# Scores of two heads as 64-row products, with the mask added on TensorE

## The chip, the cores and the metric

The kernel runs on one core of a Trainium2 chip. The metric is the device time of one launch in microseconds (us). The kernel before takes 739.22 us, the median of three runs (739.21 to 739.76).

## The reference

Local attention with a memory, and a gated MLP behind it. q, k and v are 4 batches x 8 heads x 576 tokens x 64 features, in float32.

```python
scores = q @ k.T / 8                      # causal, later keys at -1e9
local  = softmax(scores) @ v
q_p    = where(q > 0, q, exp(q) - 1) + 1
mem    = (q_p @ M_prev) / (q_p . z_prev + 1e-6)
x      = sigmoid(beta) * mem + (1 - sigmoid(beta)) * local     # 2304 x 512
out    = ((x @ w_a) * (x @ w_b)) @ w_out                       # d_ff = 1536
```

## The kernel before

Every float32 product is made of three products of split numbers: x = hi + lo, and x * y = hi * hi + hi * lo + lo * hi.

**Attention** works on a pair of heads, A and B, at a time; there are 16 pairs. The queries of a head lie in four tiles of 128 tokens (0 to 3), and the last 64 tokens of both heads share one tile (4). The work on a pair is cut into named steps, and the string `ORDER` (L21) is the order of all steps within one iteration, written by hand as `step:lag`: in iteration i a step works on pair i - lag. So an iteration holds steps of up to four pairs, and each engine runs its part of them strictly in that order. An iteration is what repeats; the first ones lack the late steps, and the last ones the early steps.

The steps that the change and the prediction touch:

- `TK`, `TQ`, `Tq` (L395) turn k and q on TensorE into feature layout; `th` (L409, ScalarE) copies the hi part out of PSUM and `tl` (L416, VectorE) the lo part. The result is `f`, with head A on partitions 0 to 63 and head B on 64 to 127: `f[0]` holds q's hi and k's lo, `f[1]` q's lo and k's hi.
- `D_` (L422) copies `f` by four DMAs into `two`, where the two parts of one head stand over each other on 128 partitions. Pair 0 has no `two`.
- `S_A`, `S_B` (tiles 0 and 1 of a head, in one PSUM bank), `S_2A`, `S_2B`, `S_3A`, `S_3B` (tiles 2 and 3) and `S_4` (L449) are the scores. A tile of a head takes one 64-row product of `f` (L459) and one 128-row product of `two` (L462), which holds the other two terms. Pair 0 takes three 64-row products. Tile 4 takes six products (L470).
- `m` (L483, VectorE) adds the mask, a bf16 tile as wide as the scores, and takes the row minimum in the same pass; the pass leaves the minimum in an accumulator, and a second short instruction reads it. Of tiles 0 and 1 the masked scores go to SBUF (tile `P`), of the others back to PSUM.
- `e` (L495, ScalarE) takes the exponential, from SBUF or PSUM, and sums it.
- `r_` and `n` (VectorE, GpSimd) scale the rows; `G` (L531, TensorE) turns the probabilities; `h`, `l` (L565, L590) split them to hi and lo; `V` (L602) multiplies them with v; `x` (L623) takes the result out.

Beside these, iterations hold steps of the memory's part of x: those of a token tile (`ma`, `mb`, `mu`, `mc`, `md`, `me`; 6 tiles, the work of VectorE) in iterations 2 to 7 and a little behind, those of a pair's features (`pa` to `py`; 8 of them, with products on TensorE) behind these.

PSUM has eight banks: six are the tiles `pt` of one pool (`ps_t`, L271), which the steps T, S, G, pa and pe take in turn, each waiting until a bank's last reader is done; two make one wide tile `pw` for S_4 and V.

**The MLP** (L736 on) follows. Its weights come as two words of a float64 and are put together by VectorE, ScalarE and GpSimd while the first columns run on TensorE; from then on TensorE works alone. The change does not touch it, but for the order of its first steps in the last iterations.

Of the kernel before, what the change touches and what calls it, by code (L numbers as in the profile page):

```python
# [22 lines left out]
S_2A:1 hi0:3 clamp2:3 S_2B:1 pf:3 cx:3 lo0:3 r_:2 V1A:3 sm:0 V2A:3 thK:0 high3:3 shift2:3 thQ:0  # L23
tlK:0 pa:2 e3A:1 ma:0 mag4:3 xA:3 Tq:0 pd:2 tlQ:0 clamp4:3 m2A:1 thq:0 mb:0 pb:2 high2:3 m2B:1
clamp1:2 S_3B:1 mag3:2 e2A:1 shift1:2 H0:3 shift4:3 S_A:1 e2B:1 m3B:1 n2:2 clamp0:2 V1B:3 low2:3
high1:2 e3B:1 mA:1 shift0:2 pc:2 V2B:3 n4:2 G2B:2 tlq:0 mx:3 S_B:1 hi2:3 G2A:2 xB:3 mu:0 md:2
n1:2 D_:0 low3:3 h2B:2 Lt:-1 high4:3 clamp3:2 h2A:2 low4:3 eA:1 n3:2 low1:2 high0:2 hi1:2
shift3:2 G5:2 n0:2 G1:2 S_4:1 lo2:3 h5:2 v_h:2 Lp:1 mB:1 h1:2 low0:2 l2B:2 G4:2 h4:2 l2A:2 Lv:1
hh:3 Lk:-2 G0:2 G3A:2 h0:2 lo1:2 v_l:2 hl:3 w_0:2 LM:0 st_:3 l0:2 h3A:2 me:2 px:3 G3B:2 h3B:2
m4:1 l5:2 py:3  # L30
# [1135 lines left out]
```

## Time and profile before

| what | before |
|---|---|
| median of three runs | 739.22 us |
| the profiled execution, first to last instruction | 736.9 us |
| what lies around that span, against the median | 2.3 us |
| TensorE busy | 706.5 us (96%), 3861 products |
| VectorE busy | 487.5 us (66%) |
| ScalarE busy | 326.9 us (44%) |
| GpSimd busy | 256.1 us (35%) |
| mean granted clock of TensorE | 0.984 |

A busy TensorE is not one at its peak: a product is shown from its start until its result has landed, and the next starts long before that. What a product takes from the engine is the distance from its start to the next one's start. Attention ends at about 230 us and its last steps at about 252 us of the span, the weights are done at about 369 us, and the rest is the MLP alone.

### The profile page before, as it was taken

The numbers are of one execution on the slowest core, as the hardware profiler recorded it, in microseconds if no ns is written. First come the engines' busy times: TensorE is split into PE (matmuls) and PEld (weight loads), VectorE is DVE, ScalarE is ACT, GpSimd is POOL, SyncE is SP. The second block draws the span as 40 slices with busy tenths as digits, with TensorE's granted clock in tenths as the row PEclk, the third lists the DMA queues.
The fourth block names the chain that finished last, engine by engine and source line by source line (L and its number), as shares of the span: only waits on it lengthen the run. The fifth ranks groups of instructions, "written<-read, shape, count | busy, mean of one in ns | idle before, by whom it ended". The sixth has DMA issues, their size and how long they took to land.

```text
span 736.9 us, 11356 instructions
## 1 busy us (share of the span) xinstructions
PE 706.5 (96%) x3861; PEld 627.2 (85%) x3861; DVE 487.5 (66%) x1128; ACT 326.9 (44%) x821; POOL 256.1 (35%) x359
## 2 busy tenths in 40 slices
PE   7999999999998897978899999999999999999998
PEld 6777778778877886878799999999999999999997
DVE  6889999877888999999966754445444454441111
ACT  5787877877777544444332222222222222221111
POOL 1687887778678533333361020000100010000000
PEclk9799999999999998999999999999999999999999
DMA  7999989989985354344214231112111121001001
GB/s 164 213 206 196 236 192 214 229 173 203 226 216 172 103 173 144 123 150 147 79 58 97 44 98 23 31 25 71 41 30 32 54 56 32 1 3 41 1 0 44
DMA packets 129465, 79.98 MB, mean 109 GB/s; under 512 B 98816, under 2 KB 117248, under 8 KB 129408
## 3 DMA queue, kind: packets, MB, share of 16 engines
q1 hardware_dynamic: 129408, 79.26, 44.4%
q8 instruction: 31, 0.51, 0.3%
q14 instruction: 26, 0.21, 0.1%
HBM read 49.35 MB, written 14.16 MB: 86 GB/s over the span
## 4 chain that ended last, share of the span: by engine, by line
PE 76%; DVE 16%; ACT 3%; issue 2%; DMA 1%; SPq 1%; POOL 1%; DVEq 0%
PE pp L840 30%; PE o L877 15%; PE pt L89 8%; PE pw L618 6%; PE pt L462 6%; PE pt L459 6%; DVE wt L778 4%; DVE wt L785 3%; DVE wt L771 3%; PE pw L470 1%; DVE wt L764 1%; PE m L1013 1%; ACT hh L859 1%; DVE hl L93 1%; POOL P L518 1%
## 5 line engine op out<-in xcount | busy, mean ns | idle before, releaser
L840 PE MATMUL pp<-xh,wh 128*128 128x384 f32 x568 | 194.1, 342 | 16.1 <-ACT x L852 15.3
L840 PE MATMUL pp<-xh,wl 128*128 128x384 f32 x568 | 192.7, 339 | 0.0
L840 PE MATMUL pp<-xl,wh 128*128 128x384 f32 x568 | 192.3, 338 | 0.0
L840 PEld LDWEIGHTS pp<-xh,wh 128*128 128x128 f32 x568 | 108.0, 190 | 23.5 <-ACT x L852 20.1
L855 DVE TENSOR_TENSOR x<-pp,x 128x384 f32<-128x384 f32 x71 | 39.3, 553 | 122.7 <-ACT x L852 122.5
L840 PEld LDWEIGHTS pp<-xl,wh 128*128 128x128 f32 x568 | 108.1, 190 | 2.6
L840 PEld LDWEIGHTS pp<-xh,wl 128*128 128x128 f32 x568 | 108.0, 190 | 0.0
L852 ACT ACTIVATE x<-pp 128x384 f32<-128x384 f32 x71 | 34.4, 484 | 124.6 <-PE pp L840 124.6
L518 POOL TENSOR_SCALAR P<-P,sum 128x384 f32<-128x384 f32 (+2 forms) x144 | 81.7, 590 | 22.2 <-DVE sum L510 21.7
L1005 POOL TENSOR_TENSOR xx<-xx 128x384 f32<-128x384 f32 x16 | 16.7, 1042 | 200.9 <-DMA xx<-xs 158.1
L877 PE MATMUL o<-wh,hl 128*128 128x512 f32 x216 | 85.5, 396 | 0.0
L877 PE MATMUL o<-wl,hh 128*128 128x512 f32 x216 | 85.0, 393 | 0.0
L877 PE MATMUL o<-wh,hh 128*128 128x512 f32 x216 | 84.9, 393 | 0.0
L93 POOL TENSOR_TENSOR wl<-wt,wh 128x512 fp32r<-128x512 f32 x32 | 45.5, 1421 | 77.4 <-DVE hl L93 39.3
L93 DVE TENSOR_TENSOR hl<-x,hh 128x384 fp32r<-128x384 f32 x71 | 40.5, 571 | 42.0 <-ACT hh L859 42.0
L859 ACT ACTIVATE hh<-x 128x384 fp32r<-128x384 f32 x72 | 37.8, 525 | 63.0 <-DVE x L855 63.0
L93 DVE TENSOR_TENSOR PT<-pt,PT 128x512 fp32r<-128x512 f32 (+2 forms) x112 | 60.7, 588 | 2.1 <-ACT PT L573 1.1
L573 ACT ACTIVATE PT<-pt 128x512 fp32r<-128x512 f32 (+2 forms) x112 | 52.6, 513 | 17.0 <-PE pt L89 17.0
L618 PEld LDWEIGHTS pw<-PT,vh 128*128 128x128 f32 x416 | 57.1, 189 | 2.0 <-POOL PT L93 1.2
L89 PE MATMUL pt<-ident,P 128*128 128x128 f32 (+1 forms) x400 | 55.5, 282 | 3.1 <-POOL P L518 3.0
L618 PE MATMUL pw<-PT,vh 128*128 128x320 f32 (+4 forms) x416 | 56.3, 285 | 1.8 <-POOL xh L251 1.0
L462 PE MATMUL pt<-two 128*128 128x128 f32 (+2 forms) x120 | 50.9, 424 | 2.3 <-DMA two<-f 2.3
(128 smaller groups left out, 1191.1 us busy)
## 6 DMA issues: line engine op xcount, KB each, us to landing
two<-f SPq DMA_DIRECT2D x60, 256.0 KB, 4.4
xs<-xo SPq DMA_DIRECT2D x16, 576.0 KB, 4.8
xx<-xs SPq DMA_DIRECT2D x48, 192.0 KB, 3.4
...
```

The lines of the kernel that those rows point to most:

```text
L89: nc.tensor.transpose(out, x, ident[0:x.shape[0], 0:x.shape[0]])
L93: eng.tensor_tensor(out=lo, in0=x, in1=hi, op=ALU.subtract)
L459: nc.tensor.matmul(o, lhsT=f[0][r, qc], rhs=f[1][r, kc], start=True, stop=False)
L462: nc.tensor.matmul(o, lhsT=t[:, qc], rhs=t[:, kc], start=False, stop=(t is lows[-1]))
L518: nc.gpsimd.tensor_scalar(out=pr[:, h, :], in0=pr[:, h, :], scalar1=r[:, c:c + 1], scalar2=1.0, op0=ALU.mult, op1=ALU.mult,)
L573: nc.scalar.activation(out=dst, in_=src, func=AF.Copy)
L618: nc.tensor.matmul(pv[:, a:hi], lhsT=w, rhs=x, start=(n == 0), stop=(n == len(ops) - 1))
L840: nc.tensor.matmul(pp, lhsT=w[:, w0:w0 + P], rhs=x[:, kk, :], start=(c == 0), stop=(c == 3 * KK - 1),)
L852: nc.scalar.activation(out=x, in_=ps[1], func=AF.Copy)
L855: nc.vector.tensor_tensor(out=h[0], in0=ps[0], in1=h[0], op=ALU.mult)
L859: nc.scalar.activation(out=h[1], in_=h[0], func=AF.Copy)
L877: nc.tensor.matmul(po[t, m], lhsT=hx[:, m * P:(m + 1) * P], rhs=w[:, w0:w0 + DM], start=(f == 0 and n == 0), stop=(f == NFT - 1 and n == 2),)
```

## The change

- A tile's scores are three 64-row products in place of one 64-row and one 128-row product, and `D_`, `two` and their DMAs are gone.
- The steps of A and B become one: `S_`, `S_2` and `S_3` make both heads' tiles, and the products alternate between A, on rows 0 to 63, and B, on rows 64 to 127. Each head's tile has its own bank, so a step takes two.
- The mask is added by a product: `ident_b` (a bf16 identity) times `mask` (128 x 128), into the last 128 columns of each tile of 0 to 3, and `mask_t` (64 columns) of tile 4.
- `m` is a plain row minimum of VectorE, read from PSUM; nothing is written back, and there is no second instruction. `e` reads all scores from PSUM.
- The order string is made anew.

```diff
 ORDER = """
-l1:3 e4:2 eB:2 l4:3 mc:1 mag2:3 pe:3 H1:3 mag1:2 l3A:3 TK:0 l3B:3 S_3A:1 mag0:2 m3A:1 TQ:0
...
+mc:1 l1:3 e4:2 l4:3 eB:2 H1:3 S_3:1 pe:3 mag1:2 l3A:3 TK:0 l3B:3 m3A:1 mag2:3 m3B:1 TQ:0 hi0:3
...
-        @steps("")
-        def D_(s, b, j, part):
-            if s is st[0]:
-                return
-            two = s["two"] = p2_e.tile([P, 2, 2 * FULL], F32R, tag="two", name="two")
-            for n in range(2):
-                for h in range(2):
-                    nc.sync.dma_start(
-                        out=two[64 * n:64 * n + 64, h, :].bitcast(F32),
-                        in_=s["f"][n][64 * h:64 * h + 64, 0:2 * FULL].bitcast(F32),
-                    )
...
-        @steps(*PARTS)
+        def add_product(o, w, x, first=False):
+            nc.tensor.matmul(o, lhsT=w, rhs=x, start=first, stop=True, skip_group_check=True)
+
+        @steps("", "2", "3")
         def S_(s, b, j, part):
...
+            f, tiles = s["f"], []
+            for h in "AB":
+                s["S", part + h] = psum()
+                tiles.append(list(scores(s, part + h)))
+                for i, *_, o in tiles[-1]:
+                    add_product(o[:, i * P:], ident_b, mask, i != 1)
+            for two in zip(*tiles):
+                for w, x in ((f[0], f[1]), (f[0], f[0]), (f[1], f[1])):
+                    for i, h, _, o in two:
+                        r = slice(64 * h, 64 * h + 64)
+                        add_product(
+                            o, w[r, i * P:(i + 1) * P], x[r, FULL:FULL + P * (i + 1)]
                         )
...
+        @steps(str(NF))
+        def S_(s, b, j, part):
+            s["S", part] = wide(S, HALF)
+            (*_, o), = scores(s, part)
+            f, qd = s["f"], s["qd"]
+            add_product(o[:, FULL:S], ident_b, mask_t, True)
...
         def m(s, b, j, part):
...
-            for i, h, c, src in scores(s, part):
-                nc.vector.tensor_tensor_reduce(
-                    out=masked(s, i, h, src), in0=src,
-                    in1=mask_t if i == NF else mask[:, FULL - (i + 1) * P:],
-                    scale=1.0, scalar=FAR, op0=ALU.add, op1=ALU.min, accum_out=s["nm"][:, c:c + 1],
-                )
...
+            for _, _, c, src in scores(s, part):
+                nc.vector.tensor_reduce(out=s["nm"][:, c:c + 1], in_=src, axis=AX.X, op=ALU.min)
...
                 nc.scalar.activation(
-                    out=s["P", i][:, h, :], in_=masked(s, i, h, src), func=AF.Exp, scale=-1.0,
+                    out=s["P", i][:, h, :], in_=src, func=AF.Exp, scale=-1.0,
                     bias=s["nm"][:, c:c + 1], accum_out=s["sum"][:, c:c + 1],
                 )
```

What the change does to the order, at three places. TensorE before, in an iteration of the middle, from the turning of the next pair's k (`kr`) on: S_3A, then the turning of q (`qr`), S_2A and S_2B, then V (`pw<-PT,vh`).

```order
L89 MATMUL pt<-ident,kr 128x128 x4
L459 MATMUL pt<-f_2634,f_2633 128x512
L462 MATMUL pt<-two 128x512
L89 MATMUL pt<-ident,qr 128x128 x4
L459 MATMUL pt<-f_2634,f_2633 128x384
L462 MATMUL pt<-two 128x384
L459 MATMUL pt<-f_2634,f_2633 128x384
L462 MATMUL pt<-two 128x384
L618 MATMUL pw<-PT_2718,vh 128x256
```

TensorE now, the same place: S_3 of both heads with its two mask products, a step of the memory (L239), k and q, and V; S_2 stands behind V.

```order
L436 LDWEIGHTS ident_b
L436 MATMUL pt<-mask,ident_b 128x128
L436 LDWEIGHTS ident_b
L436 MATMUL pt<-mask,ident_b 128x128
L436 MATMUL pt<-f_2545,f_2544 128x512 x2
L436 MATMUL pt<-f_2544 128x512 x2
L436 MATMUL pt<-f_2545 128x512 x2
L239 MATMUL pt<-nh,md_203 128x384
L239 MATMUL pt<-nl,md_203 128x384
L239 MATMUL pt<-nh,md_203 128x384
L88 MATMUL pt<-ident,kr 128x128 x4
L88 MATMUL pt<-ident,qr 128x128 x4
```

The 64-row products of a step now stand together, six at a time, where a 64-row and a 128-row product took turns; S_3A and S_3B, which stood half an iteration apart, are one step at its start.

ScalarE before, from the hi copies of the next pair's k and q (`f<-pt`) to the exponentials of tiles 0 and 1 of head A.

```order
L413 ACTIVATE f_2634<-pt 128x512
L413 ACTIVATE f_2633<-pt 128x512
L499 ACTIVATE P_2603,sum<-pt,nm 128x512
L627 ACTIVATE xo<-pw 128x576
L413 ACTIVATE f_2634<-pt 128x64
L413 ACTIVATE qdiag_102<-pt 64x64 x2
L223 ACTIVATE nh<-pt 128x384
L499 ACTIVATE P_2651,sum<-pt,nm 128x384 x2
L499 ACTIVATE P_2603,sum<-pt,nm 128x512
L627 ACTIVATE xo<-pw 128x576
L573 ACTIVATE PT_2718<-pt 128x3x128 x2
L499 ACTIVATE P_2678,sum<-P_2678,nm 128x128
```

ScalarE now, the same stretch.

```order
L412 ACTIVATE f_2769<-pt 128x512
L412 ACTIVATE f_2768<-pt 128x512
L484 ACTIVATE P_2788,sum<-pt,nm 128x512
L612 ACTIVATE xo<-pw 128x576
L484 ACTIVATE P_2788,sum<-pt,nm 128x512
L222 ACTIVATE nh<-pt 128x384
L412 ACTIVATE f_2769<-pt 128x64
L412 ACTIVATE qdiag_102<-pt 64x64 x2
L484 ACTIVATE P_2828,sum<-pt,nm 128x384 x2
L612 ACTIVATE xo<-pw 128x576
L558 ACTIVATE PT_2866<-pt 128x3x128 x2
L484 ACTIVATE P_2880,sum<-pt,nm 128x128
```

The second exponential of tile 3 (512 columns) moved ahead, and those of tiles 0 and 1 read `pt`, a PSUM bank, where they read `P` in SBUF. Next, SyncE's queue of an iteration before.

```order
L631 DMA xs<-xo 256x1x576
L428 DMA two<-f_2421 64x1024 x2
L428 DMA two<-f_2422 64x1024 x2
L211 DMA xx<-xs 64x2x384 x2
L330 DMA vr<-in_v_dram 128x4x64 x2
```

And SyncE's queue of an iteration now.

```order
L616 DMA xs<-xo 256x1x576
L329 DMA kr<-in_k_dram 128x4x64 x2
L329 DMA qr<-in_q_dram 128x4x64 x2
L210 DMA xx<-xs 64x2x384 x2
L329 DMA vr<-in_v_dram 128x4x64 x2
```

The four copies into `two` are gone, and the loads of k and q stand directly behind the store of `xo`.

## Rows read from the trace of the kernel before

**Rows 1.** Busy time by stretch, first line says what the columns are.
```profile
core 0: us, PE busy (x) PEld busy (x) DVE busy (x) ACT busy (x) POOL busy (x), PEclk, DMA share, GB/s
44.25:113.06 68.81, 68.27 (x417) 54.52 (x416) 65.15 (x182) 57.40 (x171) 57.28 (x88) 1.00 0.97 208
...
113.06:230.00 116.94, 116.17 (x721) 93.66 (x720) 95.11 (x275) 91.65 (x272) 88.84 (x146) 1.00 0.87 193
...
252.00:369.00 117.00, 101.32 (x499) 91.85 (x499) 108.53 (x157) 50.41 (x94) 43.18 (x32) 0.96 0.43 138
```
**Rows 2.** Timeline of TensorE, scores in one iteration: start us, us, engine, line, what.
```profile
173.67 0.60 PE L89 MATMUL pt<-ident,kr 128*128 128x128 f32 x4
174.20 0.49 PE L459 MATMUL pt<-f,f 64*128 64x512 f32 x1
...
174.96 0.60 PE L89 MATMUL pt<-ident,qr 128*128 128x128 f32 x4
175.49 0.44 PE L459 MATMUL pt<-f,f 64*128 64x384 f32 x1
...
176.89 0.28 PE L618 MATMUL pw<-PT,vh 128*128 128x256 f32 x1
...
183.35 0.32 PE L459 MATMUL pt<-f,f 64*128 64x128 f32 x1
...
184.40 0.27 PE L89 MATMUL pt<-ident,P 128*128 128x128 f32 x1
```
**Rows 3.** Timeline of TensorE, the scores of pair 0 (64-row products alone).
```profile
10.11 0.49 PE L459 MATMUL pt<-f,f 64*128 64x512 f32 x1
...
11.00 0.66 PE L89 MATMUL pt<-ident,qr 128*128 128x128 f32 x4
11.59 0.45 PE L459 MATMUL pt<-f,f 64*128 64x384 f32 x2
...
12.21 0.21 PE L400 MATMUL pt<-ident,kt 64*128 64x64 f32 x1
...
12.66 0.47 PE L459 MATMUL pt<-f,f 64*128 64x512 f32 x1
...
14.22 1.08 PE L470 MATMUL pw<-f,qdiag 128*128 128x288 f32 x6
```
**Rows 4.** Groups of ScalarE from 113 to 230 us: xcount, busy us, mean ns.
```profile
L627 ACT ACTIVATE xo<-pw 128x576 f32<-128x576 f32 x16 | 10.4, 651 | 16.7 <-PE pw L618 16.7
L499 ACT ACTIVATE P<-pt,nm 128x384 f32<-128x384 f32 x16 | 9.1, 580 | 0.0
L499 ACT ACTIVATE P<-P,nm 128x256 f32<-128x256 f32 x17 | 8.6, 508 | 0.0
L573 ACT ACTIVATE PT<-pt 128x384 fp32r<-128x384 f32 x16 | 7.8, 489 | 6.5 <-PE pt L89 6.5
L499 ACT ACTIVATE P<-P,nm 128x128 f32<-128x128 f32 x16 | 6.5, 404 | 0.0
```
**Rows 5.** Timeline of ScalarE, two copies of 512 columns behind each other.
```profile
173.08 1.07 ACT L573 ACTIVATE PT<-pt 128x512 fp32r<-128x512 f32 x2
```
**Rows 6.** Groups of VectorE, a masked row minimum and a row sum, both of 384 columns.
```profile
L487 DVE CUSTOM_DVE_ANT_0 pt<-pt,mask 128x384 f32<-128x384 f32 x32 | 17.3, 567 | 0.0
...
L986 DVE TENSOR_REDUCE n<-q 128x12 f32<-128x384 f32 x16 | 8.8, 553 | 0.6
```
**Rows 7.** Timeline of TensorE, pair 1's first product of `two`.
```profile
18.42 0.47 PE L462 MATMUL pt<-two 128*128 128x512 f32 x1 [2.25 <-DMA two<-f]
```
**Rows 8.** Busy time by stretch, behind that wait; columns as in group 1.
```profile
20.00:22.00 2.00, 2.00 (x6) 1.00 (x5) 2.00 (x6) 1.38 (x4) 1.74 (x3) 0.54 1.20 266
22.00:30.00 8.00, 8.00 (x25) 5.84 (x26) 6.31 (x19) 4.67 (x17) 5.76 (x11) 0.50 1.14 210
```

More of the change, by code (lines that the diff above doesn't have):

```diff
@@ L21 @@
 ORDER = """
-l1:3 e4:2 eB:2 l4:3 mc:1 mag2:3 pe:3 H1:3 mag1:2 l3A:3 TK:0 l3B:3 S_3A:1 mag0:2 m3A:1 TQ:0
[L23 to L30, printed above, removed]
+mc:1 l1:3 e4:2 l4:3 eB:2 H1:3 S_3:1 pe:3 mag1:2 l3A:3 TK:0 l3B:3 m3A:1 mag2:3 m3B:1 TQ:0 hi0:3
+clamp2:3 pf:3 lo0:3 V1A:3 V2A:3 thK:0 high3:3 S_2:1 tlK:0 thQ:0 pa:2 e3B:1 ma:0 cx:3 mag4:3
+shift2:3 xA:3 S_:1 r_:2 e3A:1 tlQ:0 clamp4:3 high2:3 m2A:1 mag0:2 pb:2 Tq:0 pd:2 thq:0 mb:0
+clamp1:2 mag3:2 shift1:2 n2:2 H0:3 px:3 shift4:3 m2B:1 e2B:1 high1:2 clamp0:2 mA:1 V1B:3 low2:3
+shift0:2 V2B:3 mB:1 n4:2 G2B:2 pc:2 hi2:3 e2A:1 tlq:0 mx:3 low1:2 G2A:2 xB:3 G5:2 mu:0 md:2 h2B:2
+n3:2 n1:2 h2A:2 clamp3:2 high0:2 low3:3 l2B:2 G1:2 high4:3 hh:3 eA:1 low4:3 shift3:2 hi1:2 n0:2
+lo2:3 v_h:2 h5:2 S_4:1 sm:-1 py:3 LM:0 Lp:1 h1:2 low0:2 G4:2 Lt:-1 h4:2 l2A:2 Lv:1 v_l:2 G0:2
+G3A:2 lo1:2 h0:2 hl:3 w_0:2 l0:2 h3A:2 st_:3 me:2 G3B:2 h3B:2 m4:1 l5:2 Lk:-2
 """
@@ L437, in attention @@
         PARTS[str(NF)] = ((NF,), 0)
+        HALF = S // 2
         def scores(s, part):
@@ L446, in scores @@
                 a += n
-        @steps(*PARTS)
+        def add_product(o, w, x, first=False):
+            nc.tensor.matmul(o, lhsT=w, rhs=x, start=first, stop=True, skip_group_check=True)
+        @steps("", "2", "3")
         def S_(s, b, j, part):
-            f, two = s["f"], s.get("two")
-            half = S // 2
-            s["S", part] = wide(S, half) if part == str(NF) else psum()
-            for i, h, _, o in scores(s, part):
-                n = o.shape[1]
-                if i < NF:
-                    qc = slice(i * P, (i + 1) * P)
-                    kc = slice(FULL, FULL + n)
-                    r = slice(64 * h, 64 * h + 64)
-                    nc.tensor.matmul(o, lhsT=f[0][r, qc], rhs=f[1][r, kc], start=True, stop=False)
-                    lows = [t[:, h] for t in (two,)] if two else [t[r] for t in f]
-                    for t in lows:
-                        nc.tensor.matmul(
-                            o, lhsT=t[:, qc], rhs=t[:, kc], start=False, stop=(t is lows[-1])
-                        )
-                    continue
-                qd = s["qd"]
-                for r in range(2):
-                    kc = slice(FULL + r * half, FULL + (r + 1) * half)
-                    for c, (w, x) in enumerate(((0, f[1]), (0, f[0]), (1, f[1]))):
-                        nc.tensor.matmul(
-                            o[:, r * half:(r + 1) * half], lhsT=qd[:, w, :],
-                            rhs=x[:, kc], start=(c == 0), stop=(c == 2),
-                        )
@@ L475, in masked @@
-        def masked(s, i, h, src):
-            if ("P", i) not in s:
-                shape = [P, 2 if i < NF else 1, src.shape[1]]
-                s["P", i] = p2.tile(shape, F32, tag=f"P{i}", name=f"P{i}")
-            return s["P", i][:, h, :] if i < 2 else src
+            f, tiles = s["f"], []
[4 more added lines that the diff above has]
+                    add_product(o[:, i * P:], ident_b, mask, i != 1)
@@ new lines, in S_ @@
+            for two in zip(*tiles):
[4 more added lines that the diff above has]
+                            o, w[r, i * P:(i + 1) * P], x[r, FULL:FULL + P * (i + 1)]
+                        )
+        @steps(str(NF))
[4 more added lines that the diff above has]
+            add_product(o[:, FULL:S], ident_b, mask_t, True)
+            for r in range(2):
+                kc = slice(FULL + r * HALF, FULL + (r + 1) * HALF)
+                for c, (w, x) in enumerate(((0, f[1]), (0, f[0]), (1, f[1]))):
+                    add_product(
+                        o[:, r * HALF:(r + 1) * HALF], qd[:, w, :], x[:, kc], r == 0 and c == 0
+                    )
@@ L498, in e @@
             for i, h, c, src in scores(s, part):
+                if ("P", i) not in s:
+                    shape = [P, 2 if i < NF else 1, src.shape[1]]
+                    s["P", i] = p2.tile(shape, F32, tag=f"P{i}", name=f"P{i}")
                 nc.scalar.activation(
-                    out=s["P", i][:, h, :], in_=masked(s, i, h, src), func=AF.Exp, scale=-1.0,
+                    out=s["P", i][:, h, :], in_=src, func=AF.Exp, scale=-1.0,
                     bias=s["nm"][:, c:c + 1], accum_out=s["sum"][:, c:c + 1],
@@ L653, in attention @@
         load_pair(1, "kq")
-        mask = p2_e.tile([P, FULL], BF16, name="mask", bufs=1)
-        mask_t = p2_e.tile([P, S], BF16, name="mask_t", bufs=1)
+        mask = p2_e.tile([P, P], BF16, name="mask", bufs=1)
+        mask_t = p2_e.tile([P, TAIL], BF16, name="mask_t", bufs=1)
+        ident_b = p2_e.tile([P, P], BF16, name="ident_b", bufs=1)
         mask_f = mem.tile([P, TPB, DM], F32, tag="ph", name="mask_f", bufs=2)[:, 0, 0:P]
         make_identity(nc, ident)
-        for t in (mask, mask_t):
-            nc.vector.memset(t, 0.0)
+        nc.vector.tensor_copy(ident_b, ident)
         make_causal_mask(nc, mask_f, mask_val=FAR)
-        nc.vector.tensor_copy(mask[:, FULL - P:], mask_f)
+        nc.vector.tensor_copy(mask, mask_f)
         for e in range(2):
             r = slice(64 * e, 64 * e + 64)
-            nc.vector.tensor_copy(mask_t[r, FULL:], mask_f[r, r])
+            nc.vector.tensor_copy(mask_t[r], mask_f[r, r])
         names = [w.split(":") for w in ORDER.split()]
```

1 line of the change is left out of this document (removed).

## The prediction, written before the changed kernel ran

> **What bounds the kernel now.** I read the busy time by stretch first. From 113 to 230 us TensorE is busy for 116.17 of 116.94 us and VectorE for 95.11; from 44 to 113 us TensorE is busy for 68.27 of 68.81 us, and VectorE, with the token tiles' work on it, for 65.15 [rows 1]. "Busy" alone would not show that TensorE is the limit, so I then read its timeline: within the scores each product starts as soon as the one before lets it, with no wait on another engine that the timeline names [rows 2]. So attention runs at TensorE's pace, at 116.94 / 8 = 14.62 us an iteration in the later stretch and 68.81 / 5 = 13.76 in the earlier one, and VectorE is close behind in the earlier one alone. From 252 to 369 us VectorE is busy for 108.53 of 117 us [rows 1]: the weights set the pace there, and the change leaves them as they are.
>
> **TensorE: scores.** Before, from a step's first product to the first start behind it, S_3A takes 174.96 - 174.20 = 0.76 us, S_2A and S_2B together 176.89 - 175.49 = 1.40, S_B 184.40 - 183.35 = 1.05 [rows 2]. S_3B and S_A are alike, which makes 0.76 x 2 + 1.40 + 1.05 x 2 = 5.0 us a pair.
>
> What the new products cost is in this trace, since pair 0 has 64-row products alone. There the two heads' first products of S_2 stand in one row of 0.45 us with x2, and all six take 12.21 - 11.59 = 0.62 us, where the two-product form takes 1.40 [rows 2, 3]: the heads run side by side. S_3A of one head, three products of 512 columns, takes 11.00 - 10.11 = 0.89 [rows 3]; with B beside A I take 0.9 for both. For S_ (twelve short products) the nearest row is the stretch 12.66 to 14.22, which holds S_3B, S_A and S_B of pair 0 in 1.56 us [rows 3]; S_ alone lies between 0.62, the six of S_2, and 1.56. I take 1.0. S_2 gets 0.1 more than 0.62, as a 128-row product follows it now. Sum: 0.9 + 0.7 + 1.0 = 2.6 us.
>
> The mask products (eight of 128 columns, one of 64) have no row. Nearest are the transposes, four of which take 174.20 - 173.67 = 0.53 us with the switch to 64 rows behind them, 0.13 each [rows 2]; so they cost from 0 (behind weights and products under way) to 9 x 0.13 = 1.2 us. I take 0.7, near the transposes, as these too are one load and one product of 128 columns. TensorE's gain is 5.0 - 2.6 - 0.7 = 1.7 us a pair, 0.6 to 2.8 by the bounds. Its work in a later iteration falls to about 12.9 us, in an earlier one to 12.0.
>
> **What is late next in the later iterations.** ScalarE. I walk one iteration from the mask products of S_3. TensorE needs about 7.4 us to the result of `Tq`: S_3 and its masks 1.15, the memory's products 0.6, k and q 0.9, V of A 1.6, S_2 1.0, a memory transpose 0.4, S_ 1.3, Tq 0.45. Then `Tq`'s hi copy starts on ScalarE, and behind it in its order stand two exponentials of 384 columns, `xo`, two copies of 384, the exponentials of tiles 0 and 1, the copies h5, h1, h4 and h0, and h0 frees the bank that the next S_3 takes. Means are 0.580, 0.651, 0.489, 0.404 and 0.508 us [rows 4]; copies overlap by 0.1 us, as two of 512 columns show, which take 1.07 us together [rows 5]. So 0.6 + 2 x 0.56 + 0.55 + 2 x 0.39 + 0.9 + 0.2 + 0.5 + 0.5 + 0.3 = 5.4 us. 7.4 + 5.4 = 12.8, and I add 0.3 for the handovers: **13.1 us**, 1.5 less than 14.62, over 8 iterations 12 us. By TensorE alone the gain would be 8 x 1.7 = 14; with a wait of half a microsecond more in each, 8.
>
> **The earlier iterations.** VectorE is next, and what it gains is small. A masked minimum of 384 columns is 0.567 us; a plain reduction of 384 columns, from SBUF, is 0.553 [rows 6], and no row shows one from PSUM. The second instruction that reads the accumulator starts together with the next pass wherever one is ready, so it was hidden already. I take 0.15 us an iteration, with 0 and 0.9 (0.1 for each of nine, the whole of that second instruction) as ends. 65.15 - 5 x 0.15 is 64.4, and with 0.2 us of waits in each of five 65.4: 68.81 - 65.4 = **3.4 us**, 0 to 5. The Trainium skill speaks against this edit (VectorE: DVE Perf Modes, Rules for kernel authors): it calls `tensor_reduce` the slowest operation of that engine, to be restructured away from a hot path. The two rows do not bear that out against the pass that goes; if it held for PSUM, this gain would be lost.
>
> **The start.** Pair 1's first product of `two` waits 2.25 us for its DMA [rows 7], and behind that stop the granted clock is 0.54 and then 0.50 of full speed, the 1.2 GHz level, until 30 us [rows 8]. With `two` gone the wait goes; but now S_2 of pair 1 must wait until all exponentials of pair 0 have left their banks, since both heads hold one each. Walking the first two iterations with the durations above, the third starts at about 28.4 us, where it starts at about 31: **2.7 us**, 0 if the clock falls all the same, 5 if it never falls.
>
> **Moves with no price.** SyncE loses the four copies into `two` each iteration and gains nothing; every load of q, k and v moves ahead, and TensorE hardly waits for any now. The exponentials of tiles 0 and 1 read PSUM: by the steps of 0.10 us from 128 to 256 columns and 0.07 from 256 (SBUF) to 384 (PSUM) [rows 4], a PSUM read costs no more. At the start one more cast (`ident_b`) hides behind the loads. The MLP is unchanged, and the end of attention, VectorE's, moves as a whole.
>
> **Sum.** 12 + 3.4 + 2.7 = 18.1 us. The profiled execution spans 736.9 us and would span 718.8; the median of the runs lies 2.3 us above the span, so I predict **721 us** (713 to 726 for this case).
>
> **Rivals.**
>
> Banks. Both heads' scores take two of six banks from their mask products on, and those of tiles 0 and 1 keep them until the exponentials, which ScalarE, busy 91.65 of 116.94 us [rows 1], may run late. TensorE, stopped at a mask product, holds back all that stands behind it, V and the transposes. With 14.0 us in place of 13.1 and half of the earlier gain, that is 721 + 7.2 + 1.7 = 730. For it: each step has two such waits now. Against it: in my walk those of the middle are met early. The Trainium skill names this price (TensorEngine Tiling, Gotcha 1: PSUM Pressure): row tiles write different banks, so packing raises the need for them.
>
> Reduction dear. A minimum from PSUM costs 0.1 us more than the masked pass: the earlier iterations gain nothing, the later ones 0.2 less each, 721 + 3.4 + 1.6 = 726.
>
> The heads do not run side by side (the change does not do what it says). Then S_3 and S_2 cost 0.65 and 0.5 us more and S_ 0.6 to 0.7; TensorE's gain of 1.7 is gone, and the start alone is left: 736. Against it: pair 0's row with x2 [rows 3].
>
> Slower: the clock. TensorE is full now; after, it stops several times in an iteration, and one stop of 2.25 us was followed by 10 us at the 1.2 GHz level [rows 7, 8]. Such 10 us do 5 us of work too little, and TensorE has almost no slack: 5 us a fall. Four falls eat the gain; one in every second of 13 iterations would give 721 + 6 x 5 = 751. [...]
>
> **Chances.** Forecast 0.62, banks 0.22, reduction 0.07, no overlap 0.05, clock 0.04. The range, 711 to 732, takes in the first three, and the ends of the mask, overlap and wait costs. All but the last are faster by over 0.2% (1.5 us, about what a measurement of this kernel can tell from no change); between faster and slower little is left, and a banks case worse than I priced it has a small share there: faster 0.93, same 0.03, slower 0.04.
>
> **What would show it.** In the profile after: iterations of about 13.1 us in the later stretch; S_2's six products within 0.7 us, two by two at one start; mask products of 0.1 us or less; ScalarE without a stop from `Tq`'s copies to h0, and TensorE waiting for it at the mask products of S_3; VectorE over 97% busy while token tiles run; no row of `two`; the clock at 1.00 from 44 us on. The prediction is wrong if TensorE waits for banks in the middle of an iteration (S_2, S_), if a minimum takes over 0.65 us for 384 columns, or if the granted clock falls in the stretch where it is 1.00 now.

## The result, and the profile after

The changed kernel takes **711.96 us**, the median of four runs (711.33 to 712.69); the kernel before, run beside it, takes 739.22. The ratio is 0.9634, with a 95% interval of 0.9622 to 0.9647. That is 27.3 us less, where the sum had 18.1. It lies in the range of 711 to 732, less than 1 us above its low end, and below the 713 to 726 that were given for the forecast's own case. The profiled execution took 711.34 us and spans 709.6.

Page of the kernel after: busy time of each engine, its share of the span and its instructions.

```profile
PE 675.5 (95%) x4125; PEld 614.1 (87%) x4125; DVE 468.4 (66%) x983; ACT 324.0 (46%) x821; POOL 255.7 (36%) x359
```

Busy time by stretch, kernel after: 44 to 113 us, 113 to 230 us, and one token-tile iteration; columns as in [rows 1].

```profile
44.00:113.00 69.00, 66.68 (x569) 57.19 (x569) 65.90 (x158) 62.72 (x191) 64.96 (x103) 1.00 0.62 152
113.00:230.00 117.00, 110.31 (x882) 97.72 (x881) 99.42 (x214) 96.18 (x270) 96.01 (x151) 0.99 0.54 146
...
79.05:91.12 12.07, 11.84 (x102) 10.08 (x100) 11.67 (x29) 11.32 (x35) 11.35 (x19) 1.00 0.51 127
```

The same view of the kernel before, for the iteration that answers to the last of these:

```profile
87.35:100.88 13.53, 13.53 (x85) 10.90 (x84) 13.04 (x38) 11.62 (x36) 11.33 (x17) 1.00 1.04 228
```

The first two rows look like [rows 1]: the same engines are nearly full (in the second row TensorE is less so, as the end of attention now lies in it). What changed is how much work lies in a stretch. The third row against the fourth shows it for one iteration: 1.46 us less, and VectorE's busy time fell by nearly as much, 1.37 us. From here on an iteration is taken from the start of one turning of k (`kr` on TensorE) to the next.

| part of the span | before | after | gain | in the sum |
|---|---|---|---|---|
| start, to the fourth `kr` | 32.03 | 29.65 | 2.4 | 2.7 |
| six iterations with token tiles | 83.06 | 73.17 | 9.9 | 3.4 |
| six later iterations | 87.81 | 77.77 | 10.0 | 9.0 (six of the eight) |
| end of attention, to the last `xo` | 49.92 | 45.44 | 4.5 | 3.0 (the other two) |
| the rest | 484.1 | 483.6 | 0.5 | 0 |

The one large miss is the second row: 6.5 of the 9.2 us by which the gain exceeds the sum.

Timeline of TensorE, kernel after: the scores of a later iteration (start us, us, engine, line, what).

```profile
141.93 0.60 PE L88 MATMUL pt<-ident,kr 128*128 128x128 f32 x4
...
144.40 0.29 PE L436 MATMUL pt<-mask,ident_b 128*128 128x128 bf16 x2
144.62 0.44 PE L436 MATMUL pt<-f,f 64*128 64x384 f32 x2
...
145.34 0.55 PE L88 MATMUL pt<-ident,ph 128*128 128x128 f32 x3
145.72 0.39 PE L436 MATMUL pt<-mask,ident_b 128*128 128x128 bf16 x4
146.04 0.33 PE L436 MATMUL pt<-f,f 64*128 64x128 f32 x2
...
146.84 0.22 PE L399 MATMUL pt<-ident,kt 64*128 64x64 f32 x1
...
152.91 0.38 PE L436 MATMUL pt<-mask,ident_b 128*128 128x128 bf16 x2
153.22 0.50 PE L436 MATMUL pt<-f,f 64*128 64x512 f32 x2
...
154.11 0.44 PE L239 MATMUL pt<-nh,md 128*128 128x384 f32 x1
...
154.74 0.60 PE L88 MATMUL pt<-ident,kr 128*128 128x128 f32 x4
```

S_2 takes 145.34 - 144.62 = 0.72 us, S_ 146.84 - 146.04 = 0.80, S_3 154.11 - 153.22 = 0.89: 2.4 us (2.6 in the sum). The mask products take 0.22 + 0.32 + 0.31 = 0.85 (0.7). So TensorE gains 5.0 - 2.4 - 0.85 = 1.75 us a pair (1.7), and the iteration takes 154.74 - 141.93 = 12.81 us (13.1).

All waits of TensorE in the six later iterations (102.82 to 180.59 us), kernel after: us in total, times, longest.

```profile
PE pt L88 <- DVE PT L92: 1.2, 6, 0.4
```

Each is a transpose that waits for VectorE's copy of the probabilities. None is for ScalarE.

Groups of VectorE, kernel after: row minima from PSUM, and the rescaling of the sums (`r_`); xcount, busy us, mean ns.

```profile
L473 DVE TENSOR_REDUCE nm<-pt 128x1 f32<-128x384 f32 x32 | 16.8, 551 | 4.1 <-PE pt L436 4.1
...
L492 DVE SCALAR_TENSOR_TENSOR sum<-sum,over_ungate 128x9 f32<-128x9 f32 x16 | 3.2, 198 | 0.0
```

A plain minimum of 384 columns from PSUM takes 551 ns, where the masked pass took 567 [rows 6]: not dear, and no great gain. `r_` has the same form as before, where its mean was 569 ns. This row set the second half of the experiments.

### The profile page after: what moved, and what is told of

Read it like the earlier page. It is cut to its first block, busy times and chain, and to the rows that moved or that the text cites. A ratio compares the mean times of both kernels' runs of the same rounds, so it can differ in the third digit from the quotient of the medians.

```text
span 709.6 us, 11536 instructions
## 1 busy us (share of the span) xinstructions
PE 675.5 (95%) x4125; PEld 614.1 (87%) x4125; DVE 468.4 (66%) x983; ACT 324.0 (46%) x821; POOL 255.7 (36%) x359
## 4 chain that ended last, share of the span: by engine, by line
PE 68%; DVE 19%; POOL 6%; ACT 3%; issue 2%; DMA 1%; SPq 0%; POOLq 0%; DVEq 0%
PE pp L825 33%; PE o L862 16%; PE pt L88 6%; DVE wt L763 5%; PE pt L436 4%; POOL P L503 4%; PE pw L603 4%; DVE wt L770 3%; DVE wt L756 3%; DVE wt L749 1%; DVE nm L473 1%; PE pw L436 1%; PE m L998 1%; DVE hl L92 1%; ACT hh L844 1%
## 5 line engine op out<-in xcount | busy, mean ns | idle before, releaser
L503 POOL TENSOR_SCALAR P<-P,sum 128x384 f32<-128x384 f32 (+2 forms) x144 | 84.2, 604 | 34.5 <-ACT P L484 16.9
L92 POOL TENSOR_TENSOR wl<-wt,wh 128x512 fp32r<-128x512 f32 x32 | 45.0, 1405 | 77.2 <-DVE hl L92 38.6
L484 ACT ACTIVATE P<-pt,nm 128x512 f32<-128x512 f32 (+3 forms) x128 | 67.1, 535 | 1.3 <-DVE nm L473 0.9
L88 PE MATMUL pt<-ident,P 128*128 128x128 f32 (+1 forms) x400 | 57.5, 283 | 8.8 <-POOL P L503 4.1
L473 DVE TENSOR_REDUCE nm<-pt 128x1 f32<-128x512 f32 (+3 forms) x128 | 55.1, 482 | 10.4 <-PE pt L436 10.3
L603 PE MATMUL pw<-PT,vh 128*128 128x320 f32 (+4 forms) x416 | 59.1, 292 | 1.7 <-ACT P L484 0.8
```

The lines of the kernel that those rows point to most:

```text
L88: nc.tensor.transpose(out, x, ident[0:x.shape[0], 0:x.shape[0]])
L92: eng.tensor_tensor(out=lo, in0=x, in1=hi, op=ALU.subtract)
L473: nc.vector.tensor_reduce(out=s["nm"][:, c:c + 1], in_=src, axis=AX.X, op=ALU.min)
L484: nc.scalar.activation(out=s["P", i][:, h, :], in_=src, func=AF.Exp, scale=-1.0, bias=s["nm"][:, c:c + 1], accum_out=s["sum"][:, c:c + 1],)
L503: nc.gpsimd.tensor_scalar(out=pr[:, h, :], in0=pr[:, h, :], scalar1=r[:, c:c + 1], scalar2=1.0, op0=ALU.mult, op1=ALU.mult,)
L603: nc.tensor.matmul(pv[:, a:hi], lhsT=w, rhs=x, start=(n == 0), stop=(n == len(ops) - 1))
```

## The experiments

My theory was the prediction's: TensorE's products set the time, VectorE is next while token tiles run. The rivals: the new order by itself, the DMAs of `D_`, or VectorE's lighter minimum carries the gain.

### Order alone, and products alone

`order_alone` is the kernel before with the new order.

```diff
-l1:3 e4:2 eB:2 l4:3 mc:1 mag2:3 pe:3 H1:3 mag1:2 l3A:3 TK:0 l3B:3 S_3A:1 mag0:2 m3A:1 TQ:0
+mc:1 l1:3 e4:2 l4:3 eB:2 H1:3 S_3A:1 S_3B:1 pe:3 mag1:2 l3A:3 TK:0 l3B:3 m3A:1 mag2:3 m3B:1 TQ:0 hi0:3
...
```

> The kernel before, with the new order alone: S_3A and S_3B stand where S_3 does, and so for the other scores; D_ stands behind n1. Scores, mask and minimum are the old ones. My theory (the products set the time): TensorE's work per pair is unchanged, so the later iterations stay at 14.4 to 14.7 us and the time at 735 to 740. Rival (the order itself gives a good part of the 27 us, by placing small steps where no other engine is in their way): 720 to 730, and the rescaling of the sums (r_) at 0.2 us in place of 0.57.

Measured: 753.74 us, ratio 1.0191 (1.0168 to 1.0214), slower than either had it. Iterations take 14.4 and 16.0 us in turn. Timeline of TensorE and busy time by stretch, `order_alone`:

```profile
144.56 0.44 PE L458 MATMUL pt<-f,f 64*128 64x384 f32 x1
144.93 0.44 PE L461 MATMUL pt<-two 128*128 128x384 f32 x1
...
148.90 3.07 PE L617 MATMUL pw<-PT,vh 128*128 128x256 f32 x13
```
```profile
148.00:150.00 2.00, 2.00 (x11) 1.66 (x11) 1.62 (x11) 0.79 (x4) 2.00 (x5) 0.79 1.03 234
150.00:152.00 2.00, 2.00 (x10) 2.00 (x10) 0.33 (x2) 0.99 (x4) 2.00 (x5) 0.50 1.06 219
```

From 144.56 to 148.64 us 64-row and 128-row products take turns, twelve of them with three transposes between. TensorE is busy all the time, and right behind, the granted clock is 0.50, the 1.2 GHz level: the thirteen products of V take 3.07 us where they take 1.85 in the kernel after. In the old order S_A and S_B stood apart and the clock was 1.00 [rows 1]. So with the old products the new order does harm.

`rows_only` is the kernel before with one edit, the products of pair 0 for all pairs.

```diff
-            f, two = s["f"], s.get("two")
+            f, two = s["f"], None
```

(`D_` is gone, from `ORDER` too.)

> The kernel before with one edit: every pair takes three 64-row products a tile, as pair 0 did, and D_ with its copies is gone. A's and B's steps, the order, mask and minimum are the old ones. Theory (no switch from 64 to 128 rows within a step, and side by side where A's and B's steps touch): TensorE's 5.0 us of scores a pair fall to 0.89 for S_3A, 0.62 for S_2, and 1.56 to 1.8 for the rest, 3.2 in all; later iterations 12.9 to 13.4, token-tile iterations held at 13.0 to 13.6 by VectorE: 721 to 727. Rival (only the paired steps with masks on TensorE make it fast): 733 to 739.

Measured: 723.08 us, ratio 0.9771 (0.9744 to 0.9799), as expected. Later iterations take 13.08 us. Sixteen of the 27 us come from this edit alone. Busy time by stretch, `rows_only`, a token-tile iteration and a later one:

```profile
85.14:97.86 12.72, 12.33 (x92) 10.45 (x92) 12.51 (x38) 11.96 (x36) 11.70 (x18) 1.00 0.47 124
178.49:191.70 13.21, 13.21 (x102) 11.41 (x101) 11.41 (x35) 11.33 (x35) 10.93 (x19) 1.00 0.47 125
```

### The new products in the old order, the old products in the new

`old_order`: the changed kernel, with S_3, S_2 and S_ where S_3A, S_2A and S_A stood.

```diff
-mc:1 l1:3 e4:2 l4:3 eB:2 H1:3 S_3:1 pe:3 mag1:2 l3A:3 TK:0 l3B:3 m3A:1 mag2:3 m3B:1 TQ:0 hi0:3
+l1:3 e4:2 eB:2 l4:3 mc:1 mag2:3 pe:3 H1:3 mag1:2 l3A:3 TK:0 l3B:3 S_3:1 mag0:2 m3A:1 TQ:0
...
```

> The changed kernel in the old order: S_3 where S_3A was, S_2 where S_2A was, S_ where S_A was, the B steps and D_ gone. Theory (the products carry the gain, and the new order only suits it): TensorE's work is the same 12.2 us, iterations at 12.8 to 13.6, 712 to 722. Rival (the old order makes the waits for banks that I feared, as S_3 takes both banks half an iteration before eB needs its own): 14 us an iteration, 726 or more.

Measured: 749.76 us, ratio 1.0132 (1.0102 to 1.0161): the rival. Timeline of TensorE and busy time by stretch, `old_order`:

```profile
151.80 0.27 PE L437 MATMUL pt<-mask,ident_b 128*128 128x128 bf16 x2 [1.61 <-ACT P L485]
...
152.89 3.17 PE L604 MATMUL pw<-PT,vh 128*128 128x256 f32 x13
```
```profile
154.00:156.00 2.00, 2.00 (x10) 2.00 (x10) 1.17 (x6) 0.00 (x0) 0.24 (x1) 0.50 0.00 0
```

Here both mishaps that I had feared stand in one place. The second head's mask product of S_ waits 1.61 us for an exponential to leave its bank (the banks), and behind this stop the clock is at 0.50 (the clock). Seven such waits make 11.2 us in the trace from 113 to 230 us, and the later iterations take 17.4 us.

`two_back`: the changed kernel with `D_` and its copies, and a 64-row and a 128-row product per tile again.

```diff
...
-            for two in zip(*tiles):
-                for w, x in ((f[0], f[1]), (f[0], f[0]), (f[1], f[1])):
...
+            for i, h, _, o in (x for y in zip(*tiles) for x in y):
...
+                add_product(o, f[0][r, qc], f[1][r, kc])
+                for t in [two[:, h]] if two else [t[r] for t in f]:
+                    add_product(o, t[:, qc], t[:, kc])
```

> The changed kernel with the four copies into two back, and with each tile of 0 to 3 as one 64-row and one 128-row product again; mask products, minimum and order as in the change. My theory: this gives TensorE its 2.4 us a pair back (5.0 against 2.6 and less), less the 0.5 us or so that TensorE now waits in an iteration: later iterations at 14.4 to 15 us, earlier ones at 13.5 to 14, 730 to 738 in all. Rival (VectorE's lighter minimum and the order carry the gain): 712 to 722.

Measured: 773.31 us, ratio 1.045 (1.043 to 1.0469), far above both. Timeline of TensorE and busy time by stretch, `two_back`:

```profile
158.79 0.33 PE L448 MATMUL pt<-f,f 64*128 64x128 f32 x1
159.04 0.33 PE L448 MATMUL pt<-two 128*128 128x128 f32 x1
...
161.06 0.27 PE L399 MATMUL pt<-ident,kt 64*128 64x64 f32 x1
...
161.34 3.28 PE L615 MATMUL pw<-PT,vh 128*128 128x256 f32 x13
```
```profile
158.50:161.10 2.60, 2.60 (x15) 1.70 (x12) 0.96 (x3) 0.49 (x1) 2.60 (x6) 1.00 1.00 257
161.10:164.40 3.30, 3.30 (x16) 3.23 (x15) 1.72 (x7) 1.78 (x7) 3.30 (x6) 0.53 1.10 205
```

S_ takes 161.06 - 158.79 = 2.27 us here, 0.80 in the kernel after; all scores 5.3 against 2.4. With 2.9 us more the iteration would be 15.7 us, and the trace has 15.5 where the clock holds. The other iterations take 17.0, with the clock at 0.53 behind S_, again with no stop ahead of it. My 730 to 738 was a miss: 2.7 us in each of some 14 iterations make 38 us, which I had put at half. The rest of 61 lies in iterations with the lower clock and in the start (38.95 us to the fourth `kr`, 29.65 in the kernel after), and was not taken apart further. So the 64-row products are what the change lives on.

### The mask on VectorE, and no mask

`mask_on_vector`: the changed kernel without mask products; `m` adds the mask and takes the minimum as before, and tiles 0 and 1 go to SBUF.

```diff
-                for i, *_, o in tiles[-1]:
-                    add_product(o[:, i * P:], ident_b, mask, i != 1)
...
-                nc.vector.tensor_reduce(out=s["nm"][:, c:c + 1], in_=src, axis=AX.X, op=ALU.min)
+                nc.vector.tensor_tensor_reduce(
+                    out=masked(s, i, h, src), in0=src,
...
```

> The changed kernel without mask products; VectorE adds the mask and takes the minimum in one pass, with its second instruction, as before. Theory A (VectorE sets the pace while token tiles run, and the nine second instructions of 0.115 us each were on its path): the six token-tile iterations go from 12.2 to 13.1 or 13.3 us, the later ones gain the mask products' 0.6 us of TensorE or part of it: 711.9 + 6 - (2 to 5) = 713 to 716. Rival (the second instructions were hidden, as I had priced them): token-tile iterations stay at 12.2, later ones gain, 705 to 710.

`no_mask` leaves the nine mask products out and puts nothing in their place.

> The changed kernel with the nine mask products left out, so that the scores are not causal; all else stands. It measures these products. If TensorE sets the pace: they and the switch to 64 rows behind them take 0.6 to 0.9 us of an iteration, 8 later iterations gain 0.5 to 0.8 each and the token-tile ones little: 704 to 708. If the chain from Tq over ScalarE to h0 sets it, as my walk had it: the later iterations stay within 0.2 us of 12.9, 710 to 712.

Measured: `mask_on_vector` 709.59 us, ratio 0.9584 (0.956 to 0.9608), **faster than the change as it was made**, by 2.4 us; `no_mask` 707.33. Busy time by stretch, a token-tile iteration and a later one of `mask_on_vector`, then a token-tile iteration of `no_mask`:

```profile
79.25:91.39 12.14, 11.50 (x93) 9.84 (x91) 11.93 (x38) 11.37 (x35) 11.28 (x17) 1.00 0.44 118
166.29:178.62 12.33, 12.28 (x103) 10.63 (x102) 10.95 (x35) 11.43 (x35) 10.88 (x19) 1.00 0.58 158
```
```profile
79.23:91.24 12.01, 11.28 (x94) 9.70 (x92) 11.80 (x29) 11.24 (x35) 11.29 (x18) 1.00 0.48 123
```

The token-tile iterations are as long as with the plain minimum (12.14 and 12.07), so the nine second instructions were hidden and theory A falls. In `no_mask` TensorE has 0.56 us less to do in such an iteration, yet the iteration takes 12.01 us for 12.07: VectorE, busy for 11.80, is the fuller engine there. The later iterations take 12.3 to 12.5 us against 12.8 to 12.9: without mask products TensorE goes faster by 0.5 us, and is busy for 12.28 of 12.33. `no_mask` has 12.2 to 12.3. These shorter iterations alone do not tell TensorE's pace from the chain over ScalarE, as I had expected them to: the walk from S_3 to `Tq` holds mask products too. The waits tell it: in the kernel after TensorE never waits for ScalarE in the later iterations, and in `mask_on_vector` from 116.72 to 178.62 us for nobody. So TensorE sets the pace there. Part of this `mask_on_vector` gives back at the start: 30.57 us at the fourth `kr`, where the change has 29.65.

### The copies alone, and the heads in turn

`copies_back`: the changed kernel with `D_` and its four DMAs, whose result nobody reads.

```diff
-n3:2 n1:2 h2A:2 clamp3:2 high0:2 low3:3 l2B:2 G1:2 high4:3 hh:3 eA:1 low4:3 shift3:2 hi1:2 n0:2
+n3:2 n1:2 D_:0 h2A:2 clamp3:2 high0:2 low3:3 l2B:2 G1:2 high4:3 hh:3 eA:1 low4:3 shift3:2 hi1:2 n0:2
```

> The changed kernel with the four copies into two back, and nobody who reads them: transfers alone. My theory (the products set the time, the transfers lie beside): 711.5 to 713. Rival (the transfers stretched VectorE's and GpSimd's work in SBUF, such as r_ at 0.57 us in place of 0.20, and that is where the earlier iterations gained more than I priced): earlier iterations at 12.8 to 13.3 us in place of 12.2, 715 to 719, and r_ back at 0.5 us or more.

Measured: 715.43 us, ratio 0.9677 (0.9662 to 0.9692), the number of the rival but not its mechanism: `r_` is at 190 ns, and the undisturbed iterations are 12.1, 12.8 and 12.9 us as without copies. Of the 4.3 us by which the profiled span is longer, 3.1 are lost in one iteration (29.37 to 44.50 us). Timelines of SyncE's queue, ScalarE and TensorE there, `copies_back`:

```profile
26.81 2.29 SPq L428 DMA_DIRECT2D two<-f  x3
...
31.10 0.61 SPq L146 DMA_DIRECT2D qr<-in_q_dram  x1
```
```profile
34.90 0.63 ACT L172 ACTIVATE ph<-qr 128x512 f32<-128x512 f32 x1 [2.76 <-DMA qr<-in_q_dram]
```
```profile
36.12 3.30 PE L615 MATMUL pw<-PT,vh 128*128 128x256 f32 x13 [1.72 <-ACT xo L624]
```

The load of a token tile's q stands behind the copies in SyncE's queue and starts at 31.10 us, where it starts at 25.93 in the kernel after; ScalarE waits 2.76 us for it with `xo` behind it, TensorE 1.72 us for `xo`, and V runs at the lower clock. In this iteration the copies' price is their place in the queue, not their traffic, which the undisturbed iterations carry at no loss.

`heads_in_turn`: all of A's products of a step, then all of B's.

```diff
-            for two in zip(*tiles):
-                for w, x in ((f[0], f[1]), (f[0], f[0]), (f[1], f[1])):
-                    for i, h, _, o in two:
...
+            for i, h, _, o in (x for y in tiles for x in y):
+                r = slice(64 * h, 64 * h + 64)
+                for w, x in ((f[0], f[1]), (f[0], f[0]), (f[1], f[1])):
...
```

> The changed kernel with all of A's products of a step first and all of B's behind them, in place of one of A, one of B. My theory (the two row halves of TensorE work side by side, whichever order the program has, as pair 0 of the kernel before hints): 711 to 714, the six products of S_2 in about 0.7 us as with alternation. Rival (products start in program order, so that only neighbours of different heads overlap): one pair of six overlaps, S_3 takes 0.65, S_2 0.5 and S_ 0.6 us more, and 13 iterations of 1.0 to 1.7 us more make 725 to 734.

Measured: 713.96 us, ratio 0.9658 (0.9645 to 0.9671), at the upper end of what my theory had. Timeline of TensorE, `heads_in_turn`:

```profile
145.60 0.45 PE L436 MATMUL pt<-f,f 64*128 64x384 f32 x2
...
146.32 0.55 PE L88 MATMUL pt<-ident,ph 128*128 128x128 f32 x3
...
147.02 0.32 PE L436 MATMUL pt<-f,f 64*128 64x128 f32 x1
...
148.10 0.21 PE L399 MATMUL pt<-ident,kt 64*128 64x64 f32 x1
```

The program has A, A, A, B, B, B, but the first row holds both heads' first products: S_2 still takes 0.72 us. S_, with six products of a head in a row, takes 148.10 - 147.02 = 1.08 in place of 0.80. So alternating is worth something in S_ alone, 0.1 us an iteration; another 0.9 us goes at the start, where the clock is 0.81 from 13 to 27 us.

### What held VectorE up before, and what that cost

Timelines of VectorE and GpSimd in one token-tile iteration of the kernel before:

```profile
90.20 0.81 DVE L507 SCALAR_TENSOR_TENSOR sum<-sum,over_ungate 128x9 f32<-128x9 f32 x1
```
```profile
89.70 1.28 POOL L184 TENSOR_TENSOR qr<-ph,zr 128x512 f32<-128x512 f32 x1
```

`r_` on nine columns takes 0.81 us and ends at 91.01, 0.03 us behind GpSimd's product, which began ahead of it. Eleven of its sixteen instances take over 0.6 us, all of them beside a product of GpSimd; where GpSimd is idle they take 0.16 or 0.17. The Trainium skill has the rule (SBUF — State Buffer, SBUF: two separate sides): a VectorE instruction with two inputs in SBUF and a GpSimd instruction that reads SBUF exclude each other for their whole length, and the one that starts second waits. These rows agree.

Only three of the eleven stand in the six token-tile iterations, the others in later ones, which run at TensorE's pace. Over the six iterations more than `r_` shrank. Groups of VectorE, kernel before (32.03 to 115.09 us), then kernel after (29.65 to 102.82): `rn` (a small step of the token tiles) and `r_`.

```profile
L190 DVE SCALAR_TENSOR_TENSOR rn<-rn,over_gate 128x8 f32<-128x8 f32 x5 | 3.7, 736 | 0.2
L507 DVE SCALAR_TENSOR_TENSOR sum<-sum,over_ungate 128x9 f32<-128x9 f32 x6 | 2.9, 488 | 0.0
```
```profile
L189 DVE SCALAR_TENSOR_TENSOR rn<-rn,over_gate 128x8 f32<-128x8 f32 x5 | 1.3, 261 | 0.2
L492 DVE SCALAR_TENSOR_TENSOR sum<-sum,over_ungate 128x9 f32<-128x9 f32 x6 | 1.2, 207 | 0.0
```

These are 4.1 us less, of the 7.6 us by which VectorE's busy time in these iterations fell (77.2 to 69.7). But in the kernel before the holds of `r_` cost no time. Busy time by stretch, two token-tile iterations in which `r_` is short, kernel before:

```profile
32.03:45.62 13.59, 13.59 (x86) 10.96 (x85) 11.40 (x35) 11.36 (x35) 10.31 (x16) 1.00 1.15 211
60.24:73.81 13.57, 13.57 (x83) 10.95 (x84) 12.34 (x38) 10.84 (x34) 11.63 (x18) 1.00 0.88 190
```

They are as long as the one shown above (13.53, with `r_` held up and VectorE busy for 13.04), and TensorE is busy throughout in all three: it set the pace there, and VectorE's busy time only looked close to it. Two others are longer (14.62 and 14.21 us) and hold `rn` at 1.21 and 1.97 us; whether `rn` makes them long is not shown.

`sums_early`: the changed kernel, with `r_` put where GpSimd is at that product.

```diff
-mc:1 l1:3 e4:2 l4:3 eB:2 H1:3 S_3:1 pe:3 mag1:2 l3A:3 TK:0 l3B:3 m3A:1 mag2:3 m3B:1 TQ:0 hi0:3
+mc:1 l1:3 e4:2 l4:3 eB:2 H1:3 S_3:1 pe:3 mag1:2 l3A:3 TK:0 l3B:3 m3A:1 r_:2 mag2:3 m3B:1 TQ:0 hi0:3
...
-shift2:3 xA:3 S_:1 r_:2 e3A:1 tlQ:0 clamp4:3 high2:3 m2A:1 mag0:2 pb:2 Tq:0 pd:2 thq:0 mb:0
+shift2:3 xA:3 S_:1 e3A:1 tlQ:0 clamp4:3 high2:3 m2A:1 mag0:2 pb:2 Tq:0 pd:2 thq:0 mb:0
```

> The changed kernel with r_, VectorE's rescaling of the sums, moved ahead of m3B, where GpSimd is at the product of a token tile (L183, about 1.29 us, from 0.99 us behind the start of an iteration). Theory (a VectorE instruction with two operands in SBUF stands still until GpSimd's instruction is done): r_ takes 0.7 to 1.1 us in the token-tile iterations in place of 0.16, ending 20 to 30 ns behind GpSimd's product, and as VectorE sets the pace there, five or six iterations lose 0.5 to 0.8 us each: 714.5 to 717. Rival (r_ is short wherever it stands, and was long before for another reason): 0.2 us, 711.5 to 712.5.

Timelines of VectorE and GpSimd, `sums_early`:

```profile
80.37 0.73 DVE L492 SCALAR_TENSOR_TENSOR sum<-sum,over_ungate 128x9 f32<-128x9 f32 x1
```
```profile
79.79 1.29 POOL L183 TENSOR_TENSOR qr<-ph,zr 128x512 f32<-128x512 f32 x1
```

Measured: `r_` at 0.73 us in three token-tile iterations, which take 12.58, 12.56 and 12.25 us where the change has 12.16, 12.07 and 11.70: 0.4 to 0.55 us each. `r_` is held up as the theory has it, but these losses are not `r_`'s alone: in the first two the copy of a token tile (L175) takes 0.81 and 0.80 us for 0.44 and 0.47, and in the third `rn` takes 1.10 for 0.25. The whole time is 711.77 us, ratio 0.9621 (0.9605 to 0.9637), no loss and the rival's number: two others grew shorter (12.24 for 12.92, 12.86 for 13.49), for a reason that is not shown. The expected time was a miss.

`sums_late` is `rows_only` with `r_` 1 us later.

```diff
-S_2A:1 hi0:3 clamp2:3 S_2B:1 pf:3 cx:3 lo0:3 r_:2 V1A:3 sm:0 V2A:3 thK:0 high3:3 shift2:3 thQ:0
-tlK:0 pa:2 e3A:1 ma:0 mag4:3 xA:3 Tq:0 pd:2 tlQ:0 clamp4:3 m2A:1 thq:0 mb:0 pb:2 high2:3 m2B:1
+S_2A:1 hi0:3 clamp2:3 S_2B:1 pf:3 cx:3 lo0:3 V1A:3 sm:0 V2A:3 thK:0 high3:3 shift2:3 thQ:0
+tlK:0 r_:2 pa:2 e3A:1 ma:0 mag4:3 xA:3 Tq:0 pd:2 tlQ:0 clamp4:3 m2A:1 thq:0 mb:0 pb:2 high2:3 m2B:1
```

> The kernel rows_only (the one before, with 64-row products alone) with r_ moved behind tlK, some 1 us later, where GpSimd has no work while it waits for these sums. Theory (VectorE held up by GpSimd's two-operand product): r_ falls from 0.6 us to 0.16 to 0.2, and the token-tile iterations, at 12.3 to 12.7 in the undisturbed ones, go to 12.0 to 12.4; the later ones, TensorE's, stay at 13.1: 720 to 723 against 723.1. Rival (the scaling n of GpSimd starts later by the same time and holds up the transposes): 723 to 727.

Measured: 720.75 us (718.65 to 724.92), ratio 0.976 (0.9731 to 0.9788), whose interval holds that of `rows_only` for the most part: inconclusive. `r_` fell to 0.16 us in most iterations, but now another two-operand instruction, `rn`, stands beside GpSimd's work in four iterations (0.56 us, 0.17 when free), and the token-tile iterations take 12.9 us.

### The start

The kernel before stops for 2.25 us for its DMA [rows 7]. `rows_only` has neither `two` nor its DMAs, and stops at nearly the same place for VectorE's part of `f`. Timeline of TensorE, `rows_only`:

```profile
20.19 0.81 PE L446 MATMUL pt<-f,f 64*128 64x512 f32 x2 [2.09 <-DVE f L93]
```

Its clock is at 0.50 from 20 to 28 us. In `mask_on_vector` TensorE stops for 2.13 us before S_ of pair 1, and the clock is at 0.63 and 0.50 from 22 to 28. `fill_stop` puts eight products that change nothing in front of S_, `fill_ahead` in front of S_2.

```diff
+            if part == "2" and s is st[1]:
+                for _ in range(8):
+                    add_product(s["S", "2A"], ident_b, mask, True)
```

> The kernel mask_on_vector with eight products of 512 columns (bf16) that change nothing, before S_ of pair 1, in the stop of 2.13 us behind which its granted clock was 0.63 and 0.50 from 22 to 28 us. Theory (the mask products kept the clock up at the start, and this was worth more to the changed kernel than it gained from them later): the clock stays at 1.00, the third iteration starts at 28.5 to 29.5 us in place of 30.6, 706.5 to 708.5 against 709.6, the fastest of all. Rival (the start waits for ScalarE and the loads whatever the clock): 709 to 710.

> As fill_stop, but with the eight products ahead of S_2 of pair 1, whose bank is free, so that they take 1.6 to 1.8 us out of the stop of 2.13 us in place of standing behind it. Theory (the stop makes the clock fall): the clock stays at 1.00 from 13 to 30 us, the third iteration starts at 28.5 to 29.7 us in place of 30.6 and 31.5, 707 to 708.5. Rival (S_2 comes late for ScalarE and VectorE, which are full there): 709 to 711 whatever the clock does.

Measured: 709.02 us, ratio 0.9594 (0.9574 to 0.9614), and 709.79, ratio 0.9592 (0.9579 to 0.9605): no change against 0.9584. In `fill_stop` (the same, for S_ and its bank) the eight stood behind the stop, as they waited for VectorE to leave that bank. In `fill_ahead` they filled it. Timeline of TensorE and busy time by stretch, `fill_ahead`:

```profile
16.57 1.89 PE L436 MATMUL pt<-mask,ident_b 128*128 128x512 bf16 x8
...
19.59 0.75 PE L436 MATMUL pt<-f,f 64*128 64x128 f32 x2 [0.40 <-DVE f L92]
```
```profile
24.00:26.00 2.00, 1.80 (x7) 1.40 (x8) 1.34 (x3) 1.51 (x7) 2.00 (x4) 0.50 1.14 216
```

The stop is 0.40 us, and the clock falls from 22 us on all the same. My theory of this fall is refuted. In the kernel after the clock is 1.00 from 13 to 27 us, with TensorE busy for 10.71 of those 14 us and stops of up to 0.99 us. What decides at the start stays open.

## Why the prediction was right, and where it was off

- **TensorE's term held.** 1.75 us a pair against 1.7. `rows_only` and `two_back` show that the products make it.
- **"What is late next in the later iterations. ScalarE."** This step failed. The walk from `Tq` to h0 gave 13.1 us and had TensorE wait for ScalarE at the mask products of S_3; the trace has 12.8 to 12.9 and no such wait. TensorE is still the limit, and nearly its whole gain arrives: 10.0 us in six iterations, of 6 x 1.75 = 10.5, where the sum had 9.0.
- **"The earlier iterations. VectorE is next, and what it gains is small."** This is the mis-sized term: 3.4 us in the sum, 9.9 measured, outside the 0 to 5 that it was given. VectorE is next indeed, as `no_mask` suggests, and the minimum is worth nothing there, by `mask_on_vector`. What failed was to take 65.15 us of busy time [rows 1] as work that stays: the sum let an iteration fall to 65.4 / 5 = 13.1 us, and it fell to 12.2. VectorE's busy time shrank by 7.6 us over six iterations, 4.1 of them in two instructions that had stood beside GpSimd, so that TensorE's lighter products could be gained almost whole. The products in the old order (`rows_only`) bring the undisturbed iterations from 13.5 to 12.3 and 12.7 us, the paired steps in the new order (`mask_on_vector`) to 12.1. How much of that last step is VectorE's shorter stands and how much other waits is not shown: `sums_early` puts `r_`'s stand back in three iterations and loses 0.4 to 0.55 us in each, but other instructions moved with it. Also, six such iterations stand where I counted five.
- **The start** was near in size (2.4 against 2.7), in part by luck. The clock never fell, for which I had put 5 us; instead TensorE stands several times for ScalarE, VectorE and GpSimd, up to 0.99 us. And the fall that I laid to the DMA's stop of 2.25 us [rows 7, 8] comes without that DMA in `rows_only`, and with a stop of 0.40 in `fill_ahead`.
- **The total** stayed in the range by less than 1 us. The range was made from the ends of mask, overlap and waits, and the miss lies in another term, so this is luck in part.
- **"The MLP is unchanged"** held: 0.5 us.
- **The rivals.** Heads not side by side: refuted, by the timeline after and by `heads_in_turn`. Reduction dear: refuted, 551 ns. The clock did not come in the changed kernel, and waits for banks at mask products only at the start (1.2 us in all), but both are real: `old_order` shows a wait of 1.61 us and the 1.2 GHz level behind it. I gave them 0.22 and 0.04 without seeing that it is the new order that keeps them away. Nor did I see that the order would harm the old products: alone it costs 14.5 us.
- **Mask on TensorE** was priced well on TensorE (0.85 us against 0.7) but not set against what it buys. It buys nothing in the token-tile iterations, costs 0.5 us in each later one, and with the mask on VectorE the kernel is 2.4 us faster.
